# First batch's softmax in four pieces: a bank for each broadcast product, scaling and exp row by row

## The chip, the cores and the metric

The kernel runs on one core of a Trainium2 chip. The metric is the device time of one execution in microseconds (us). TensorE is called PE here, VectorE DVE, ScalarE ACT, GpSimd POOL.

## The reference

Cross-covariance attention over channels, then a gated feed-forward layer. Sizes: 4 batches of 6016 tokens with 256 channels, feed-forward width 1536.

```python
qn = q / (norm(q, axis=1) + 1e-6);  kn = k / (norm(k, axis=1) + 1e-6)
s = kn.transpose(0, 2, 1) @ qn / tau          # 256 x 256 per batch, tau = 1
a = softmax(s, axis=-1)
x = (v @ a).reshape(-1, 256)
out = (sigmoid(x @ w_gate) * (x @ w_val)) @ w_out
```

## The kernel before

The kernel never forms x. It multiplies the softmax matrix into w_gate and w_val once per batch (the twelve "gh products" below, giving the weights G and H) and feeds v to those. For batches 1 to 3 all this runs beside the feed-forward matmuls of the batch before. For the first batch nothing is there to hide it: its softmax is a relay between engines, at about 35 us, right after the last q and k have been loaded.

```python
def spread_k(b):                      # norms of k, as a row on all partitions
    s["rk"] = pso.tile([P, C], FP32, tag="o", name="ps_rk")     # one PSUM bank
    for j in range(CB):               # CB = 2 blocks of 128 columns
        mm(s["rk"][:, ds(j * P, P)], s["r"][:, CB + j : CB + j + 1].to_broadcast([P, P]), ident_f, True, True)

def scale_k(b, i):                    # DVE: both norms at once
    for j in range(CB):
        x = s["x"][:, j, ds(i * P, P)]
        nc.vector.scalar_tensor_tensor(out=x, in0=x, scalar=s["r"][:, j : j + 1],
            in1=s["rk"][:, ds(i * P, P)], op0=ALU.mult, op1=ALU.mult)

def exps(b, i):                       # ACT: one exp of 256 columns per block
    nc.scalar.activation(out=e, in_=s["x"][:, :, ds(i * P, P)], func=ACT.Exp, bias=shift)
...
busy(3); spread_k(0); busy(1); scale_k(0, 0); scale_k(0, 1)
transpose_v(0, 0, ...); exps(0, 0); exps(0, 1); nc.scalar.copy(*late.pop())
sums(0, 0)                            # PE: row sums; DVE: reciprocal
gh(0, 0, psg, "g", act=False)         # even products read w_gate, odd ones w_val
gh(0, 1, psv, "v", act=True)
sums(0, 1, pss, "s")
gh(0, 2, psg, "g", act=False); gh(0, 3, psv, "v", act=True)
gh(0, 4, pso, "o", act=False)
...
for f in range(FC):                   # first chunk of the feed-forward
    glu(0, 0, f)                      # PE: ps_gate, ps_val
    if f < len(gh_order) - 5:
        gh(0, 5 + f, pso, "o")        # two banks, also used by ps_rk
```

`busy` issues matmuls that nobody reads; they keep PE running. Cuts are marked by "...".

## Time and profile before

| | before |
|---|---|
| time, median of 3 | 831.61 us (831.45 to 831.82) |
| span of the profiled execution | 829.8 us |
| first ps_rk record starts | 35.26 us |
| first ps_gate starts | 39.45 us, 4.19 after ps_rk |
| last eviction on DVE starts | 826.14 us, 790.88 after ps_rk |

The last three rows are times in the trace. I count from the first ps_rk record, because what lies ahead of it (when the last k tile lands) differs by some tenths between executions and has nothing to do with the change. The lines of gh product 0, of the first ps_gate and of the last eviction (start, length, engine, line, operation):

```profile
37.25 0.38 PE L88 MATMUL ps_gh<-w_gate,e_sb 128*128 128x512 bf16 x1
...
39.45 0.75 PE L88 MATMUL ps_gate<-vT,gh_G 128*128 128x512 bf16 x2
...
826.14 0.42 DVE L437 COPY out_sb<-ps_o 128x256 f32<-128x256 f32 x1 [0.89 <-PE ps_o L88]
```

Two things in this trace that the prediction doesn't show turned out to matter. The first are instructions in order of time at 42 us (start, length, engine, line, operation):

```profile
42.40 0.69 ACT L364 ACTIVATE gh_G<-ps_gh,rrow 128x512 bf16<-128x512 f32 x1
42.46 0.74 DVE L366 TENSOR_SCALAR gh_H<-ps_gh,rrow 128x512 bf16<-128x512 f32 x1
42.63 0.59 PE L88 MATMUL ps_val<-vT,gh_H 128*128 128x512 bf16 x2
...
43.25 0.59 PE L88 MATMUL ps_gh<-w_val,e_sb 128*128 128x512 bf16 x2
```

A pair of such matmuls follows the pair before it 0.43 us later when PE waits for nothing. Gh product 7 (the last line) could have started at 42.63 + 0.43 = 43.06. It started at 43.25, right after the DVE eviction of product 5 ended (42.46 + 0.74 = 43.20): a bubble of 0.19 us that no list of waits shows. The second is the issue of the first load of w_val, on POOL's queue:

```profile
30.68 0.71 POOL L139 DMA_DIRECT2D w_val<-in_moe_w_val_dram  x1 [0.51 <-DMA q_sb<-in_q_dram]
```

It takes 6.8 us from issue to landing, so it lands at 37.48. Product 1, which reads it, starts at 37.68. The load has 0.2 us to spare.

### The profile page before, as it was taken

Reading aid. Unit: us, or ns where it says so; the run is one execution under the profiler, and the core shown is the slowest. Engines: PE = TensorE matmul, PEld = TensorE weight load, DVE = VectorE, ACT = ScalarE, POOL = GpSimd, SP = SyncE. Lnnn points to the kernel's source line nnn. Section 1 sums busy time; section 2 is a strip of 40 time slices with the busy share of each in tenths; the row PEclk is TensorE's granted clock in tenths of the full one; section 3 lists DMA queues with packets and bytes.
Section 4 is the critical chain, followed back from the end, with each engine's and each line's share of the span. In section 5 each row is a group of like instructions: output and inputs, shape, how many; then the busy total and the mean of one; then the engine's idle time right before and its main releaser. Section 6 shows DMA issues by size and latency. Waiting matters only on the chain.

```text
span 829.8 us, 13778 instructions
## 1 busy us (share of the span) xinstructions
PE 816.5 (98%) x5210; PEld 503.4 (61%) x5224; DVE 580.9 (70%) x998; ACT 391.0 (47%) x642; POOL 83.2 (10%) x159
## 2 busy tenths in 40 slices
PE   7899999999999999999999999999999999999998
PEld 4546666666666666665576666666566566666666
DVE  6677777777667777777767777777766666666664
ACT  4554444445644444444654444444555444444442
POOL 5532100002110100000210020000000000000000
PEclk9999999999999999999999999999999999999999
DMA  9999723326755543223874453233222323322111
GB/s 209 206 206 185 134 52 90 50 62 128 138 105 104 102 108 60 53 52 82 158 140 99 84 110 78 51 77 65 61 59 64 72 51 83 70 49 70 46 36 71
DMA packets 78739, 77.19 MB, mean 93 GB/s; under 512 B 50768, under 2 KB 55632, under 8 KB 78672
## 3 DMA queue, kind: packets, MB, share of 16 engines
q0 software_dynamic: 23920, 38.81, 28.3%
q1 hardware_dynamic: 54608, 36.97, 17.1%
q8 instruction: 41, 0.67, 0.3%
q10 hardware_dynamic: 144, 0.52, 0.2%
q14 instruction: 26, 0.21, 0.1%
HBM read 78.64 MB, written 24.64 MB: 124 GB/s over the span
## 4 chain that ended last, share of the span: by engine, by line
PE 95%; DMA 3%; issue 0%; POOL 0%; DVE 0%; ACT 0%; POOLq 0%; ACTq 0%
PE ps_o L88 30%; PE ps_gate L88 29%; PE ps_val L88 29%; PE ps_s L88 4%; DMA k_sb<-in_k_dram 3%; PE ps_gh L88 2%; PE ps_n L88 0%; POOL q_sb L97 0%; PE ps_busy L88 0%; DVE hT L411 0%; PE ps_rk L88 0%; DVE x_sb L296 0%; ACT g_sb L410 0%; POOL k_sb L97 0%; ACT e_sb L309 0%
## 5 line engine op out<-in xcount | busy, mean ns | idle before, releaser
L411 DVE TENSOR_TENSOR hT<-ps_val,g_sb 128x512 bf16<-128x512 f32 (+1 forms) x576 | 391.2, 679 | 214.9 <-ACT g_sb L410 209.7
L410 ACT ACTIVATE g_sb<-ps_gate 128x512 bf16<-128x512 f32 (+1 forms) x576 | 338.2, 588 | 386.7 <-PE ps_gate L88 378.4
L88 PE MATMUL ps_gate<-vT,gh_G 128*128 128x512 bf16 (+1 forms) x1152 | 337.7, 375 | 0.6 <-ACT g_sb L410 0.4
L88 PE MATMUL ps_val<-vT,gh_H 128*128 128x512 bf16 (+1 forms) x1152 | 337.5, 375 | 0.1
L88 PE MATMUL ps_o<-w_out_sb,hT 128*128 128x256 bf16 x2256 | 326.2, 273 | 0.0
L88 PEld LDWEIGHTS <-hT 128*128 128x128 bf16 x2256 | 220.7, 98 | 124.8
L88 PEld LDWEIGHTS <-gh_H 128*128 128x128 bf16 x1152 | 112.7, 98 | 131.0 <-issue 0.4
L88 PEld LDWEIGHTS <-gh_G 128*128 128x128 bf16 x1152 | 112.4, 98 | 38.0 <-issue 0.6
L106 POOL DMA_DIRECT2D v_sb<-in_v_dram x48 | 25.6, 533 | 624.1 <-DMA vT<-v_sb 501.2
L437 DVE COPY out_sb<-ps_o 128x256 f32<-128x256 f32 x188 | 77.6, 413 | 13.5 <-PE ps_o L88 13.5
L88 PE MATMUL ps_s<-k_sb,q_sb 128*128 128x256 bf16 x376 | 66.0, 272 | 6.1 <-DMA k_sb<-in_k_dram 4.4
L88 PEld LDWEIGHTS <-q_sb 128*128 128x128 bf16 x376 | 36.6, 98 | 14.7 <-issue 6.8
L215 DVE TENSOR_TENSOR acc<-acc,sq 128x1024 bf16<-128x1024 bf16 (+1 forms) x66 | 44.1, 669 | 0.0
L176 DVE TENSOR_TENSOR sq<-q_sb 128x1024 bf16<-128x1024 bf16 (+2 forms) x44 | 29.3, 667 | 2.6 <-DMA q_sb<-in_q_dram 2.6
L97 POOL DMA_DIRECT2D q_sb<-in_q_dram x48 | 26.5, 551 | 15.2 <-DMA q_sb<-in_q_dram 6.5
L97 POOL DMA_DIRECT2D k_sb<-in_k_dram x48 | 26.3, 547 | 13.8 <-DMA k_sb<-in_k_dram 10.2
L176 DVE TENSOR_TENSOR sq<-k_sb 128x1024 bf16<-128x1024 bf16 (+2 forms) x34 | 22.4, 658 | 0.9 <-ACT sq L174 0.9
L364 ACT ACTIVATE gh_G<-ps_gh,rrow 128x512 bf16<-128x512 f32 x21 | 14.4, 687 | 12.4 <-PE ps_gh L88 8.5
L174 ACT ACTIVATE sq<-k_sb 128x1024 bf16<-128x1024 bf16 (+1 forms) x11 | 11.2, 1018 | 14.7 <-DMA k_sb<-in_k_dram 11.9
L88 PE MATMUL ps_busy<-ones_wide,ones_bf 128*128 128x512 bf16 x57 | 16.1, 408 | 1.7 <-DVE shift L127 1.6
L366 DVE TENSOR_SCALAR gh_H<-ps_gh,rrow 128x512 bf16<-128x512 f32 x22 | 16.4, 743 | 1.6 <-PE ps_gh L88 1.6
L460 DVE TENSOR_TENSOR acc<-acc,sq 128x1024 bf16<-128x1024 bf16 x16 | 11.1, 692 | 5.7 <-ACT sq L174 5.4
(58 smaller groups left out, 114.7 us busy)
## 6 DMA issues: line engine op xcount, KB each, us to landing
out_dram<-out_sb SPq DMA_DIRECT2D x44, 512.0 KB, 2.9
v_sb<-in_v_dram POOLq DMA_DIRECT2D x44, 256.0 KB, 3.9
q_sb<-in_q_dram POOLq DMA_DIRECT2D x43, 256.0 KB, 7.0
k_sb<-in_k_dram POOLq DMA_DIRECT2D x43, 256.0 KB, 7.8
out_dram<-out_sb SPq DMA_DIRECT2D x4, 384.0 KB, 2.5
w_gate<-in_moe_w_gate_dram POOLq DMA_DIRECT2D x3, 256.0 KB, 6.8
w_val<-in_moe_w_val_dram POOLq DMA_DIRECT2D x3, 256.0 KB, 7.4
w_out_sb<-in_moe_w_out_dram POOLq DMA_DIRECT2D x1, 768.0 KB, 12.6
```

The source lines that it names most:

```text
L88: nc.tensor.matmul(out, lhsT=lhsT, rhs=rhs, start=start, stop=stop, **kw)
L97: nc.gpsimd.dma_start(out=tl[:, :nt, :], in_=rows(src, b)[:, t0 : t0 + nt, :])
L106: nc.gpsimd.dma_start(out=v_sb[:, :nt, :], in_=rows(v, b)[:, t0 : t0 + nt, :])
L174: nc.scalar.activation(out=sq[:, :nt, :], in_=src[:, :nt, :], func=ACT.Square)
L176: engine.tensor_tensor(out=sq[:, :nt, :], in0=src[:, :nt, :], in1=src[:, :nt, :], op=ALU.mult)
L215: nc.vector.tensor_tensor(out=acc[:, :nt, :], in0=acc[:, :nt, :], in1=st[b]["sq", w][:, :nt, :], op=ALU.add)
L364: nc.scalar.activation(out=dst, in_=ps, func=ACT.Copy, scale=r)
L366: nc.vector.tensor_scalar(out=dst, in0=ps, scalar1=r, scalar2=None, op0=ALU.mult)
L410: nc.scalar.activation(out=g_sb[:, :n], in_=ps_gate[:, :n], func=ACT.Sigmoid)
L411: nc.vector.tensor_tensor(out=hts[b, ci][:, f, :n], in0=ps_val[:, :n], in1=g_sb[:, :n], op=ALU.mult)
L437: nc.vector.tensor_copy(out=out_sb[:, s, :], in_=ps)
L460: nc.vector.tensor_tensor(out=acc[w], in0=acc[w], in1=sq[w], op=ALU.add)
```

## The change

Intent: let DVE begin when the first half of the broadcast is there, and ACT when the first of four scalings is there. Each block's broadcast goes to a bank of its own; DVE multiplies by k's norms alone (tensor_tensor), and q's norm becomes the scale operand of an exp of 128 columns.

```diff
-    def spread_k(b):
-        s["rk"] = pso.tile([P, C], FP32, tag="o", name="ps_rk")
-        for j in range(CB): mm(s["rk"][:, ds(j * P, P)], ...)
+    def spread_k(b, i, pl, tag):
+        ps = pl.tile([P, P], FP32, tag=tag, name="ps_rk")
+        mm(ps, s["r"][:, CB + i : CB + i + 1].to_broadcast([P, P]), ident_f, True, True)
+        s.setdefault("rk", []).append(ps)
...
-    def scale_k(b, i): ...            # scalar_tensor_tensor, two norms
+    def weights(b, i):
+        e = attp.tile([P, CB, P], BF16, tag=f"e{i}", name=f"e_sb{i}", bufs=2)
         for j in range(CB):
+            y = attp.tile([P, P], FP32, tag=f"y{i}{j}", name="y_sb")
+            nc.vector.tensor_tensor(
+                out=y, in0=s["x"][:, j, ds(i * P, P)], in1=s["rk"][i], op=ALU.mult
+            )
+            nc.scalar.activation(
+                out=e[:, j, :], in_=y, func=ACT.Exp, bias=shift, scale=s["r"][:, j : j + 1]
+            )
...
-    spread_k(0)
+    spread_k(0, 0, pso, "o")
+    spread_k(0, 1, pso, "o")
     busy(1)
-    scale_k(0, 0); scale_k(0, 1)
+    weights(0, 0); weights(0, 1)
...
-    exps(0, 0); exps(0, 1)
```

(The diff is cut and its short lines are joined; the calls that it moves are all shown.)

More of the change, by code (lines that the diff above doesn't have):

```diff
@@ L270, in norms_inv @@
             )
-    def spread_k(b):
+    def spread_k(b, i, pl, tag):
         s = st[b]
-        s["rk"] = pso.tile([P, C], FP32, tag="o", name="ps_rk")
-        for j in range(CB):
-            mm(
-                s["rk"][:, ds(j * P, P)],
-                s["r"][:, CB + j : CB + j + 1].to_broadcast([P, P]),
-                ident_f,
-                True,
-                True,
-            )
+        ps = pl.tile([P, P], FP32, tag=tag, name="ps_rk")
+        mm(ps, s["r"][:, CB + i : CB + i + 1].to_broadcast([P, P]), ident_f, True, True)
+        s.setdefault("rk", []).append(ps)
     def copy_s(b, j):
@@ L289, in copy_s @@
         nc.vector.tensor_copy(out=s["x"][:, j, :], in_=s["s"][:, j, :])
-    def scale_k(b, i):
+    def weights(b, i):
         s = st[b]
+        e = attp.tile([P, CB, P], BF16, tag=f"e{i}", name=f"e_sb{i}", bufs=2)
         for j in range(CB):
-            x = s["x"][:, j, ds(i * P, P)]
-            nc.vector.scalar_tensor_tensor(
-                out=x,
-                in0=x,
-                scalar=s["r"][:, j : j + 1],
-                in1=s["rk"][:, ds(i * P, P)],
-                op0=ALU.mult,
-                op1=ALU.mult,
-            )
+            y = attp.tile([P, P], FP32, tag=f"y{i}{j}", name="y_sb")
+            nc.vector.tensor_tensor(
+                out=y, in0=s["x"][:, j, ds(i * P, P)], in1=s["rk"][i], op=ALU.mult
+            )
+            nc.scalar.activation(
+                out=e[:, j, :], in_=y, func=ACT.Exp, bias=shift, scale=s["r"][:, j : j + 1]
+            )
+        s.setdefault("e", []).append(e)
+        s.setdefault("rrow", [])
     def exps(b, i):
@@ L482 @@
     busy(3)
-    spread_k(0)
+    spread_k(0, 0, pso, "o")
+    spread_k(0, 1, pso, "o")
     busy(1)
-    scale_k(0, 0)
-    scale_k(0, 1)
+    weights(0, 0)
+    weights(0, 1)
     late = []
@@ L490 @@
     )
-    exps(0, 0)
-    exps(0, 1)
     nc.scalar.copy(*late.pop())
```

## The prediction

> **What bounds the kernel now.** I read the page first, then the chain of waits over the stretch that the change touches, then the list of instructions in order of time there, and last the list of who waited for whom on TensorE over the rest of the run. From the page, the busy shares and the line of TensorE in 40 slices:
> ```profile
> PE 816.5 (98%) x5210; PEld 503.4 (61%) x5224; DVE 580.9 (70%) x998; ACT 391.0 (47%) x642; POOL 83.2 (10%) x159
> ...
> PE   7899999999999999999999999999999999999998
> ...
> PEclk9999999999999999999999999999999999999999
> ```
> The reader is to see that TensorE (PE) is busy for 98% of the span at the full granted clock. Only the first two slices (some 41 us) have room. The edited code runs once, for the first batch; batches 1 to 3 take their softmax through other functions, hidden beside the matmuls of the batch before. So the question is what the few tenths of a microsecond around 35 to 38 us are worth. The chain of waits there, in order of time (start, length, what):
> ```profile
> 34.49 0.67 PE ps_busy L88 x3
> 35.16 0.10 issue
> 35.26 0.69 PE ps_rk L88 x4
> 35.95 0.02 issue
> 35.98 0.62 DVE x_sb L296 x2
> 36.59 0.03 issue
> 36.62 0.52 ACT e_sb L309
> 37.13 0.05 issue
> 37.18 0.20 PE ps_r L88 x2
> ```
> Read it as a relay: the broadcast product (four PE records, two passes for each of two fp32 matmuls), two of the four scalings on VectorE (DVE), the first exp on ScalarE (ACT), then the row sums on PE. The instructions in order of time add what the engines beside the chain do:
> ```profile
> 34.72 1.28 ACT L478 ACT_TABLE_LOAD   x1
> ...
> 35.98 1.12 DVE L296 SCALAR_TENSOR_TENSOR x_sb<-x_sb,r,ps_rk 128x128 f32<-128x128 f32 x4 [0.56 <-PE ps_rk L88]
> ...
> 36.62 1.02 ACT L309 ACTIVATE e_sb<-x_sb,shift 128x256 bf16<-128x256 f32 x2 [0.62 <-DVE x_sb L296]
> 37.02 0.41 DVE L385 COPY vT<-ps_tp 128x512 bf16<-128x512 bf16 x1
> ...
> 37.18 0.20 PE L88 MATMUL ps_r<-ones_bf,e_sb 128*128 128x1 bf16 x2 [0.58 <-ACT e_sb L309]
> ```
> DVE idles 0.56 us for the whole broadcast, ACT 0.62 us for the scalings, PE 0.58 us for the exp. Taken from 34.4 us to the end, the list of waits on PE has two entries only:
> ```profile
> PE ps_r L88 <- ACT e_sb L309: 0.6, 1, 0.6
> PE ps_gate L88 <- ACT g_sb L410: 0.4, 1, 0.4
> ```
> The second (at 52.4 us) hangs on ACT and DVE work that itself starts from this softmax. No DMA is in the list. So I expect whatever is won at 37.18 to go through to the end nearly whole.
>
> **What the Trainium skill says.** "ScalarE: Activation LUTs", section What ACT_TABLE_LOAD costs: an activation with immediate scale and bias takes 186 ns + 0.833 ns an element, each per-partition pointer operand adds about 93 ns, back-to-back ones overlap by about 93 ns, a load takes 1283 ns. The trace agrees: the exp of 256 columns with a pointer bias should take 492 ns and its rows say 492 to 509; both loads near here last 1.28 us; the copy behind the second exp starts at 37.55, 0.09 before that exp's end at 37.64. "VectorE: DVE Perf Modes", section The TRN2 errata: an fp32 tensor_tensor takes (N+151)/0.96 ns. The trace has none of 128 columns, but the 512-column one from PSUM should take 691 ns and shows 689. "PSUM — Partial Sum Buffer", section PSUM bank collisions raise a hardware error: PSUM is guarded by bank. Here both halves of the broadcast share a bank, and the first scaling starts 0.03 us after the last of the four PE records. "Perfetto Trace Analysis", section Optimizing Scalar/DVE Operations: "If Scalar/Vector aren't saturated, but are causing bubbles on other engines, breaking up instructions may allow work to be completed sooner." That is this change's intent; whether the pieces pay is the sum below.
>
> **The change, part by part.** (1) *A bank per block.* The first DVE instruction needs two PE records, not four. They start at 35.26 and the last at 35.67, so some 0.14 apart; the second starts near 35.40 and, at 275 ns, ends at 35.67. DVE, which finished its copy of the scores at 35.42, starts at 35.70 in place of 35.98: **-0.28**. The same matmuls are issued, so PE's work is unchanged.
>
> (2) *tensor_tensor for scalar_tensor_tensor.* The old one shows 341 ns for 128x128, four in 1.12 us, so starts 0.26 apart. The new one by the skill's formula: (128+151)/0.96 = 291 ns, and I take starts 0.25 apart (estimates). The four run 35.70-35.99, 35.95-36.24, 36.20-36.49, 36.45-36.74. The old four ended at 37.10. DVE's next work, its half of the transposed v, comes 0.3 us earlier, off the path.
>
> (3) *Exp row by row.* The scale of q's norm moves from DVE into the exp, as a second pointer. An exp of 128 columns with two pointers: 186 + 93 + 93 + 107 = 479 ns (estimate by the skill's figures), and a queue of them starts every 479 - 93 = 386 ns. The first can start once its piece is there (35.99 + 0.03) and once the table load is done (34.72 + 1.28 = 36.00): 36.02, almost a tie. So ACT runs 36.02-36.50, 36.41-36.89, 36.79-37.27, 37.18-37.66.
>
> (4) *What PE sees.* The first block of exp values is ready at 36.89, not 37.13; with the same 0.05 the row sums start at 36.94, not 37.18: **-0.24**. The relay's terms are -0.28 (bank), -0.32 (one scaling ahead of the first exp, with no second one and a shorter one) and +0.36 (two small exps take 0.87 in place of one of 0.51). The second block is ready at 37.66 against 37.64, 0.02 later; PE wants it after the row sums and four products of the first, at 38.11 - 0.24 = 37.87. So it still waits for nobody there.
>
> (5) *What follows on ACT and DVE.* ACT's half of the transposed v starts at 37.57 (was 37.55) and leaves ACT free at 38.04; the next eviction on ACT started at 38.31, so it is wanted at 38.07: just in time. DVE is done with its copy near 37.1, in time for the reciprocal of the row sums at 37.18. The step that bounds PE next is the eviction of gh_G on DVE (weights of ps_gate waited 0.48 us for it at 39.81); all of that chain starts from the row sums and moves with them. Then the sigmoid table load and everything after move by the same 0.24.
>
> Sum: 831.61 - 0.24 = 831.37; I say **831.4 us**, a gain of 0.03%.
>
> **The rivals.** *ACT takes the bound.* Exp work on ACT grows from 1.02 to 1.64 us, and step 5 leaves 0.03 us of room. If the two pointers cost more, or exps do not overlap, each exp costs 0.09 more in the queue: the first block is ready at 36.98 (-0.15), the second at 37.94, later than PE wants it, and the eviction of the second product is late by some 0.3. Then the gain is nil or a loss of 0.1 to 0.2: 831.6 to 831.8. For it: ACT has no slack here. Against it: the overlap of 0.09 is visible in this trace. *The wait isn't split.* If DVE still starts at 35.98, the first exp starts at 36.30 and the block is ready at 37.17: 0.04 later than now, time 831.6 to 831.7. For it: the table load forbids an exp before 36.00, so part of any earlier start is useless; against it: two tiles in two buffers have separate waits. *A transfer swallows it.* Between 30 and 60 us the DMA engines are busy all the time at 205 GB/s, and the next batch's q and k are read by PE from 58.3 us on. If one of those lands with less than 0.24 us to spare, PE waits and the gain is gone: 831.6. For it: DMA is full until about 83 us. Against it: PE waits for no DMA after 34.4 us, and a load of k lands in 11 us at worst while it is issued about 20 slots of 1.3 us ahead. *More is won*: up to 0.4 if DVE's pieces start closer together and the small exps are shorter than I reckon; the table load stops it there.
>
> **Range and chances.** The three runs before span 0.37 us, more than the gain, so noise in a median (some 0.15) and the rivals weigh alike. Rivals put the time between 831.2 and 831.8; with noise I take **830.9 to 831.8**. A change of 2% would be 16.6 us; all the softmax of the first batch, from the scores' end to the row sums, is about 3 us. So within 2%: 0.99, and 0.005 on each side.
>
> **What the profile of the changed kernel would show.** The broadcast's first reader on DVE at about 35.70 by the clock of the old trace (0.44 after the first ps_rk), and no wait of 0.56. Four TENSOR_TENSOR of about 290 ns. Four exps of about 480 ns, starts 0.39 apart, the first right behind the table load. The idle time of PE ahead of ps_r down from 0.58 to about 0.34, and ps_gate earlier by as much. The list of waits on PE else unchanged. I am wrong if the exps last over 0.55, if the wait for the second block or for the eviction behind it shows up on PE, or if a DMA enters that list; and the arrival of the last k tile (31.64 in this trace) can move by more than the gain from run to run, so that the total may not show what the stretch shows.

## The result, and the profile after

| | before | changed |
|---|---|---|
| time, median of 6 runs each | 831.65 us (831.45 to 831.92) | 831.39 us (831.28 to 832.01) |
| row sums done, product 0 starts, after ps_rk | 1.99 | 1.80 |
| first ps_gate, after ps_rk | 4.19 | 4.02 |
| product 7 starts, after ps_rk | 7.99 | 7.69 |
| ps_gate behind the stall at 52 us, after ps_rk | 17.16 | 16.86 |
| last eviction starts, after ps_rk | 790.88 | 790.58 |

The ratio is 0.9998 with a 95% interval of 0.9985 to 1.0011: the same, within 2% and within noise. (Ratios are the mean time of one kernel's fast runs over that of the other's of the same rounds, so not quite the ratio of the medians.) The total alone can't show a gain of this size. The traces can: from the start of ps_rk to the last eviction the changed kernel is 0.30 us shorter, and a second profile of it, taken later, gave 790.57, 0.01 off the first. From the stall at 52 us to the last eviction each of these executions takes 773.72 us, before and after, to 0.01. The lines of the changed kernel (its first ps_rk record starts at 35.30):

```profile
37.10 0.59 PE L88 MATMUL ps_gh<-w_gate,e_sb 128*128 128x512 bf16 x2
...
39.32 0.73 PE L88 MATMUL ps_gate<-vT,gh_G 128*128 128x512 bf16 x2
...
825.88 0.42 DVE L432 COPY out_sb<-ps_o 128x256 f32<-128x256 f32 x1 [0.89 <-PE ps_o L88]
```

The chain of waits of the changed kernel, in order of time (start, length, what):

```profile
35.30 0.47 PE ps_rk L88 x2
35.78 0.02 issue
35.80 0.30 DVE y_sb L291
36.10 0.02 issue
36.12 0.89 ACT e_sb L294 x2
```

Set beside the chain of the kernel before: two ps_rk records in place of four, one scaling in place of two, two small exps (0.89) in place of one wide one (0.52). The instructions in order of time:

```profile
34.76 1.28 ACT L473 ACT_TABLE_LOAD   x1
...
35.80 0.88 DVE L291 TENSOR_TENSOR y_sb<-x_sb,ps_rk 128x128 f32<-128x128 f32 x4 [0.33 <-PE ps_rk L88]
...
36.12 1.65 ACT L294 ACTIVATE e_sb<-y_sb,shift,r 128x128 bf16<-128x128 f32 x4
...
37.06 0.18 PE L88 MATMUL ps_r<-ones_bf,e_sb 128*128 128x1 bf16 x1 [0.21 <-ACT e_sb L294]
```

DVE's wait for the broadcast fell from 0.56 to 0.33. ACT's first exp starts at 36.12, behind a table load that ended at 36.04, so the load doesn't bind, but nearly. Row sums now wait for each row by itself: the first of the two ran at 36.67, in the shadow of the second exp.

The second group of lines is the one around gh product 7, and it holds what the prediction did not have:

```profile
42.25 0.69 ACT L359 ACTIVATE gh_G<-ps_gh,rrow 128x512 bf16<-128x512 f32 x1
42.33 0.74 DVE L361 TENSOR_SCALAR gh_H<-ps_gh,rrow 128x512 bf16<-128x512 f32 x1
42.48 0.59 PE L88 MATMUL ps_val<-vT,gh_H 128*128 128x512 bf16 x2
...
42.99 0.59 PE L88 MATMUL ps_gh<-w_val,e_sb 128*128 128x512 bf16 x2
```

Product 7 starts at 42.99, before the DVE eviction of product 5 ends (43.07), and 0.05 after the ACT eviction of product 6 ends (42.94). So it no longer waits for product 5. The built programs say why: before, product 7 is in the bank of product 5 (both in bank 4) and its matmul waits on DVE; after, it is in the bank of product 6 (both in bank 4, product 5 in bank 5) and waits on ACT. The code of these products is the same. The buffer allocator chose otherwise because the instructions ahead of them changed. The bubble fell from 0.19 to 42.99 - (42.48 + 0.43) = 0.08.

So 0.30 us are 0.19 from the softmax (product 0: 1.99 to 1.80) and 0.11 from a bank that moved by accident. The experiments test both.

### The profile page after: what moved, and what is told of

It is laid out like the page before. It is cut to its first block, busy times and chain, and to the rows that moved or that the text cites. A ratio compares the mean times of both kernels' runs of the same rounds, so it can differ in the third digit from the quotient of the medians.

```text
span 829.6 us, 13793 instructions
## 1 busy us (share of the span) xinstructions
PE 817.8 (99%) x5224; PEld 503.6 (61%) x5224; DVE 581.1 (70%) x998; ACT 391.9 (47%) x644; POOL 83.3 (10%) x159
## 4 chain that ended last, share of the span: by engine, by line
PE 95%; DMA 3%; POOL 0%; issue 0%; ACT 0%; DVE 0%; POOLq 0%; ACTq 0%
PE ps_o L88 30%; PE ps_val L88 29%; PE ps_gate L88 29%; PE ps_s L88 4%; DMA k_sb<-in_k_dram 3%; PE ps_gh L88 3%; PE ps_n L88 0%; PE ps_busy L88 0%; POOL q_sb L97 0%; ACT e_sb L294 0%; DVE hT L406 0%; ACT g_sb L405 0%; POOL k_sb L97 0%; PE ps_rk L88 0%; PE ps_tp L376 0%
```

## The experiments

My theory after the result: (a) the softmax part gains by the separate bank alone; the row split with two pointer operands gives a little back; (b) the rest is the bubble ahead of product 7; (c) both reach the end in full, unless a load of weights is late. Rivals: the row split carries the gain; the later stall swallows the bubble; a transfer bounds the run. Each kernel was correct, except the one that was wrong on purpose. Before measured 831.57 (first four), 831.80 (next four) and 831.71 us (last three).

| run | median us (low to high) | product 0 | product 1 | ps_gate | bubble ahead of product 7 | last eviction |
|---|---|---|---|---|---|---|
| before | 831.65 (831.45-831.92) | 1.99 | 2.42 | 4.19 | 0.19 | 790.88 |
| changed | 831.39 (831.28-832.01) | 1.80 | 2.24 | 4.02 | 0.08 | 790.58 |
| one bank | 832.27 (831.47-833.01) | 2.01 | 2.44 | 4.22 | 0.08 | 790.79 |
| banks only | 831.65 (831.26-832.83) | 1.76 | 2.25 | 4.03 | 0 | 791.04 |
| before, free bank | 831.46 (831.19-831.54) | 1.98 | 2.41 | 4.19 | 0 | 790.69 |
| delay | 833.18 (833.03-833.27) | 1.72 | 2.15 | 3.92 | 0.08 | 790.49 |
| one pointer, scaling on DVE | 831.58 (831.38-831.68) | 1.67 | 2.22 | 3.99 | 0.22 | 790.68 |
| no shift | 831.34 (831.23-832.07) | 1.61 | 2.23 | 4.00 | 0 | 790.46 |
| changed, free bank | 831.32 (831.26-831.40) | 1.79 | 2.25 | 4.02 | 0 | 790.49 |
| no shift, later products | 832.60 (832.35-833.76) | 1.61 | 2.24 | 4.02 | 0 | 791.74 |
| other weights (wrong) | 831.22 (one execution) | 1.60 | 2.03 | 3.95 | 0.08 | 790.41 |
| gate first | 831.22 (831.07-831.69) | 1.60 | 2.62 | 3.96 | 0 | 790.52 |
| changed, again | 831.35 (831.24-831.71) | 1.79 | 2.25 | 4.03 | 0.07 | 790.57 |

All columns but the first count from the first ps_rk record.

### One bank: the separate bank undone

```diff
-        ps = pl.tile([P, P], FP32, tag=tag, name="ps_rk")
+        if i == 0:
+            s["rk_both"] = pl.tile([P, C], FP32, tag=tag, name="ps_rk")
+        ps = s["rk_both"][:, ds(i * P, P)]
```

> The changed kernel with one part undone: both broadcast products again in one bank; tensor_tensor and four row exps stay. Times are counted from the start of the first ps_rk record. Before: first scaling 0.72, row sums' end-gating start 1.92, first ps_gate 4.19. Changed: 0.50, 1.76 (second ps_r), 4.02. Theory (the separate bank is the only part that gains, the row split gives some back): first scaling 0.72, first exp 1.03, second ps_r 1.95, ps_gate 4.20 to 4.23, i.e. nothing is left of the gain there. Rival (the row split gains by itself): ps_gate clearly under 4.1. Total: theory within 0.2 of before, some 0.2 us over the changed kernel, too small to be told from one total alone.

Measured: first scaling 0.72, first exp 1.04, second row sum 1.97, ps_gate 4.22. The theory holds: with one bank nothing is left of the softmax gain, and the row split by itself costs 0.02 to 0.03. The last eviction is still 0.09 earlier than before, because product 7 had the bank of product 6 here too (bubble 0.08).

Its total, 832.27, is misleading. Two of its four runs took 833.01 us, the other two 831.47 and 831.53. The profiled one is a slow one. The view of stretches shows busy time of each engine, then PEclk, the granted clock of TensorE:

```profile
core 0: us, PE busy (x) PEld busy (x) DVE busy (x) ACT busy (x) POOL busy (x), PEclk, DMA share, GB/s
28.00:31.50 3.50, 2.46 (x43) 1.85 (x42) 1.65 (x3) 1.06 (x1) 1.95 (x3) 1.00 1.16 202
31.50:35.00 3.50, 3.25 (x28) 2.33 (x29) 0.71 (x2) 2.10 (x3) 3.22 (x5) 0.52 1.23 204
35.00:40.00 5.00, 4.39 (x43) 2.69 (x43) 3.38 (x14) 3.82 (x8) 2.78 (x5) 1.00 1.24 205
```

For 3.5 us the clock was halved, and 1.5 us were lost between the last k and ps_rk (5.06 us apart, against 3.57 in other runs). That lies ahead of the edited code. A run of before (833.07, mean clock 0.998), one of banks only (832.83, 0.998) and one of no shift, later products (833.76, 0.997) look the same by time and mean clock; no trace of them was kept. The Trainium skill, "TensorE: Matmul & The Clock Gate", section What's actually happening, describes a gate with two states, half and full clock, that follows PE's activity over windows of some 3.4 us; the half clock and the length agree with this trace (a mean clock of 0.52 over 3.5 us).

### Banks only: the separate bank alone

```diff
-            y = ...; nc.vector.tensor_tensor(out=y, ...)
-            nc.scalar.activation(out=e[:, j, :], in_=y, func=ACT.Exp, bias=shift, scale=...)
+            nc.vector.scalar_tensor_tensor(out=x, in0=x, scalar=s["r"][:, j : j + 1], in1=s["rk"][i], ...)
+        nc.scalar.activation(out=e, in_=s["x"][:, :, ds(i * P, P)], func=ACT.Exp, bias=shift)
```

> The kernel before with one part of the change alone: a bank for each broadcast product; scalings with both factors and exps of 256 columns as before. Counted from the first ps_rk. Theory: first scaling 0.50, exp 1.14, row sums 1.70, so 0.05 earlier than in the changed kernel (second ps_r 1.76); then the DVE copy of the transposed v (until about 1.96) holds the reciprocal of the row sums, so ps_gate about 3.97 to 4.02, as good as the changed kernel. Rival (the row-by-row exps carry the gain): ps_gate near 4.19. The product of gh number 7 is given the bank of number 5 here, so the bubble ahead of it (about 0.19 in the kernel before, 0.08 in the changed one) should be 0.15 or more, and the total some 0.1 over the changed kernel: 831.4 to 831.6.

Measured: first scaling 0.50, exp 1.14, row sums 1.70, product 0 at 1.76, ps_gate 4.03. The bank alone gives all of the softmax gain: its row sums are even 0.06 ahead of the changed kernel's second one, and ps_gate is the same to 0.01. The rival (ps_gate near 4.19) is out. (ps_gate cannot rank the two kernels, because in both the first load of w_val sets it, as the no-shift run shows. Product 0 comes before that load matters: 1.76 here, 1.80 in the changed kernel.) The bubble forecast was missed for a reason that taught more. The list of waits on PE had an entry that no other run had:

```profile
PE ps_gh L88 <- DMA w_val<-in_moe_w_val_dram: 0.4, 1, 0.4
```

The second load of w_val took 8.1 us to land here (7.4 before), and product 5 waited for it. That gave the evictions ahead of product 7 time, so there was no bubble, and the last eviction came at 791.04. A transfer had swallowed the gain in this execution.

### Before with a free bank for product 7

```diff
-                    gh(0, 5 + f, pso, "o")
+                    gh(0, 5 + f, *((psm, "m") if f == 2 else (pso, "o")))
```

> The kernel before with only one thing changed: product number 7 of the gh weights goes to a bank that is free (that of the norms) in place of one whose eviction it waits for. Theory of the second term (in the changed kernel this product got another bank from the allocator, and the bubble ahead of it fell from 0.19 to 0.08): bubble gone, everything behind it 0.19 earlier, so the PE start behind the stall at 52.4 comes 0.19 earlier, counted from ps_rk, and the total 0.2 lower, 831.45. Rival (the bubble is swallowed by the later stall at 52.4 us, which hangs on ACT): the start behind that stall doesn't move, total as before.

Measured: ps_gate 4.19 as before, no bubble, ps_gate behind the stall at 16.97, last eviction at 790.69: exactly 0.19 less than before. The bubble is real and worth its whole length, and the later stall doesn't swallow it. The changed kernel had got 0.11 of this without asking.

### A known delay

```diff
-    busy(3)
+    busy(13)
```

> The changed kernel with ten idle 512-column products more ahead of the broadcast, 2.13 us of PE work that nobody reads: the relay is made later by a known amount. Theory (all that is won or lost ahead of ps_gate goes through to the end): ps_gate, the start behind the stall at 52.4 and the end 2.1 us later, total 833.5. Rival (a transfer or another wait behind it limits the run): total clearly under 833, and if DMA had been just in time, the list of waits on PE would have a DMA entry that vanishes.

Measured: 833.18 us, 1.79 over the changed kernel, not 2.1. From the last k to ps_gate the trace has 9.38 us against 7.59, so 1.79 later; the last eviction is 795.95 after the last k against 794.15, so 1.80. What is lost ahead of ps_gate reaches the end one for one; that every gain does is not shown by this run. The missing 0.34 is where PE had been waiting. In the changed kernel the three idle products start at 34.39, and at 0.215 each PE could have gone on at 35.04; ps_rk starts at 35.30, as the reciprocal that it reads ends at 35.16. So 0.26 of the delay filled a wait. Another 0.08 came back behind it: with PE kept busy the second ps_rk record ends earlier, and the first scaling starts 0.42 after ps_rk, not 0.50.

### One pointer, scaling on DVE

```diff
-            nc.vector.tensor_tensor(out=y, in0=..., in1=s["rk"][i], op=ALU.mult)
-            nc.scalar.activation(out=e[:, j, :], in_=y, func=ACT.Exp, bias=shift, scale=...)
+            nc.vector.scalar_tensor_tensor(out=y, in0=..., scalar=s["r"][:, j : j + 1], in1=s["rk"][i], ...)
+            nc.scalar.activation(out=e[:, j, :], in_=y, func=ACT.Exp, bias=shift)
```

> The changed kernel with the scale by q's norm moved back into DVE (scalar_tensor_tensor) while the exps stay row by row, now with one pointer operand (the shift). Theory (a pointer costs some 0.09 each on ACT, 341 against 283 ns on DVE): exp 0.39 long, the four in about 1.28 us instead of 1.65; from ps_rk: second ps_r near 1.60 against 1.76. But DVE's four scalings and its copy of v then last until about 1.96, so the reciprocal starts there, at the same 1.96 as in the changed kernel, and ps_gate stays at 4.00 to 4.03. Rival (only the exps count): ps_gate near 3.86.

Measured: exps of 386 ns in place of 480, so a pointer operand costs 94 ns. ps_gate came at 3.99 as forecast, but not for the forecast reason. The reciprocal already started at 1.87. PE had product 0 at 1.67, and could have had product 1 at 2.10, but started it at 2.22. Something else held it, which the next run shows. Beside banks only (product 0 at 1.76) this run adds the row split alone, with one pointer in each exp as there: product 0 comes 0.1 earlier. So the split does gain where it adds no second pointer. The last eviction is 0.10 later than in the changed kernel all the same: product 7 started 0.05 after the DVE eviction of product 5 had ended, as in the kernel before.

### No shift

```diff
-                out=e[:, j, :], in_=y, func=ACT.Exp, bias=shift, scale=s["r"][:, j : j + 1]
+                out=e[:, j, :], in_=y, func=ACT.Exp, scale=s["r"][:, j : j + 1]
```

> The changed kernel without the shift in the four exps (softmax is unchanged by it; scores here are at most 1), so one pointer, the scale. Theory: exp 0.39 long, starts 0.295 apart; from ps_rk: second ps_r near 1.56, DVE's copy done near 1.80, reciprocal there, ps_gate near 3.85, 0.17 under the changed kernel; total 831.2 if the second load of w_val has landed, else PE waits for that load (as one profile of the banks-only kernel showed, 0.41) and the gain is lost behind ps_gate. Rival (pointers cost nothing): as the changed kernel, second ps_r 1.76 and ps_gate 4.02.

Measured: product 0 at 1.61, 0.19 earlier than in the changed kernel, just as reckoned; product 1 at 2.23 and ps_gate at 4.00, only 0.02 earlier. PE in order of time, and the issue of the first load of w_val in the same execution:

```profile
30.55 0.71 POOL L139 DMA_DIRECT2D w_val<-in_moe_w_val_dram  x1 [0.52 <-DMA q_sb<-in_q_dram]
...
36.76 0.59 PE L88 MATMUL ps_gh<-w_gate,e_sb 128*128 128x512 bf16 x2
37.38 0.59 PE L88 MATMUL ps_gh<-w_val,e_sb 128*128 128x512 bf16 x2
```

The two pairs are 0.62 apart, not 0.43. The load lands 6.8 us after its issue, at 37.35, and the product starts 0.03 later. In the changed kernel the same load lands at 30.71 + 6.8 = 37.51, and product 1 starts at 37.54, just when PE gets there (37.10 + 0.43). So the change used up the 0.2 us that this load had to spare. In the traces of one pointer, banks only, later products, changed with a free bank and changed again, too, product 1 starts 0.03 after this landing, and in all of these, as before the change, ps_gate comes 1.77 to 1.78 after product 1. In this order of the products no faster softmax moves ps_gate while this load stays where it is.

A further limit stands behind it, and no list of waits shows it. Product 7 has no bubble here, but ps_val of the step before it starts at 42.29, where 41.74 + 0.43 = 42.17 was possible (its ps_gate pair starts at 41.74):

```profile
39.62 1.28 ACT L495 ACT_TABLE_LOAD   x1
...
41.55 0.69 DVE L406 TENSOR_TENSOR hT<-ps_val,g_sb 128x512 bf16<-128x512 f32 x1 [1.44 <-ACT g_sb L405]
...
42.29 0.59 PE L88 MATMUL ps_val<-vT,gh_H 128*128 128x512 bf16 x2
```

It starts 0.05 after DVE has read the ps_val of two steps before (41.55 + 0.69 = 42.24), DVE waited for the sigmoid on ACT, and that for its table load. The traces of one pointer, later products and gate first show the same 0.05. This link is read from the times; no run tests it alone. In the changed kernel the same DVE read ends at 42.41 and ps_val starts at 42.48, so it has 0.02 to spare.

### Changed kernel with a free bank for product 7

The edit is the one made to the kernel before.

> The changed kernel with product number 7 of the gh weights in a bank that is free. Theory: the bubble of 0.08 left ahead of it goes, the start behind the stall at 52.4 comes 16.78 after ps_rk in place of 16.86, and the last eviction 790.50 in place of 790.58. The kernel before gained 0.19 by the same edit, so with it in both, the softmax part alone is left: 790.69 - 790.50 = 0.19. Rival (the term of 0.13 comes from elsewhere): last eviction at 790.58 as in the changed kernel.

Measured: 790.49. With the bubble gone from both kernels, 790.69 - 790.49 = 0.20 is the softmax part alone, where 0.19 was forecast.

### No shift, later products: a miss

```diff
-                if (b, ci) == (0, 0) and f < len(gh_order) - 5:
-                    gh(0, 5 + f, pso, "o")
+                if (b, ci) == (0, 0) and 1 <= f <= len(gh_order) - 5:
+                    gh(0, 4 + f, pso, "o")
```

> Without the shift, and with products 5 to 11 of the gh weights each one step of the feed-forward later, so that the load of w_val has one more microsecond to land and each eviction more time. Theory (the load and the eviction are the next waits): no DMA entry in the waits on PE, no bubble ahead of product 7; last eviction after ps_rk 790.58 - 0.17 - 0.08 = 790.33, total about 831.1. Rival (the new order opens another wait on ACT or DVE): more than 790.58.

Measured: 832.60 us (832.35 to 833.76); the last eviction 791.74 after ps_rk, 1.16 later than in the changed kernel. The rival was right. Waits on PE:

```profile
PE ps_val L88 <- DVE gh_H L361: 1.3, 2, 0.7
```

Moving the products moved their evictions too, and the feed-forward now waits on DVE for weights that it needs at once. The second load of w_val, with 0.06 us to spare in the no-shift trace (landed 4.80 after ps_rk, read by product 5 at 4.86), now had 0.9; the first, which held product 1, held it here too (2.24). So nothing was won and a worse wait came.

### Other weights

```diff
-                w_sb[w][fg][:, j, :],
+                w_sb[0 if (b, n) == (0, 1) else w][fg][:, j, :],
```

> The kernel without the shift, with the first product of the val weights reading the gate weights instead (wrong numbers on purpose), so that it no longer waits for the first load of w_val. In the kernel without the shift that product starts 2.23 after ps_rk though PE is ready at 2.04; the load was issued at 30.55 and landed 6.8 us later, 37.35, and the product started at 37.38. Theory (that load is what the softmax runs into next): the product starts at 2.04 to 2.06, ps_gate at 3.82 to 3.86 in place of 4.00. Rival (PE waits there for a bank or for DVE): 2.23 and 4.00 as before.

On top of no-shift; its numbers are wrong (relative error 0.29). One execution, 831.22 us. PE in order of time, a little later:

```profile
38.12 0.59 PE L88 MATMUL ps_gh<-w_val,e_sb 128*128 128x512 bf16 x2
38.69 0.59 PE L88 MATMUL ps_gh<-w_gate,e_sb 128*128 128x512 bf16 x2
```

Product 1 now runs straight behind product 0 (the trace merges them), and the row sums of the second block come 2.46 after ps_rk, against 2.66. So it was that load. But ps_gate came at 3.95, not 3.82 to 3.86. The lines are products 3 and 4: product 4 could have started at 38.55 and started at 38.69. It reads the second load of w_gate, issued at 31.84 and landed 6.8 us later, at 38.64. The next load holds PE as the one before did: the weights arrive about as fast as PE takes them.

### Gate products first, and the changed kernel again

```diff
     gh(0, 0, psg, "g", act=False)
-    gh(0, 1, psv, "v", act=True)
     sums(0, 1, pss, "s")
     gh(0, 2, psg, "g", act=False)
+    gh(0, 1, psv, "v", act=True)
```

> The kernel without the shift, with the two gate products of both blocks ahead of the two val products, so that the first load of w_val has 0.5 us more to land. Right numbers. Theory: no gap ahead of the first val product; ps_gate at 3.90 to 3.95 after ps_rk in place of 4.00 (some is lost as the second block of exps is wanted 0.6 earlier), last eviction 790.36 to 790.42 in place of 790.46, unless the next load (the second of w_gate or w_val, each 1.25 us after the one before) holds PE instead: then 4.00 again, and that shows that the arrival of the weights paces this stretch. Total 831.2 to 831.3.

> The changed kernel again, in the same rounds as the gate-first kernel, to compare the two and to have a second profile: last eviction 790.58 after ps_rk if nothing but the arrival of k moves between executions; total 831.3 to 831.5, with single executions 1 to 1.5 us longer where the granted clock of TensorE falls in the first 35 us.

Measured in the same rounds: the table's last two rows. There is no gap ahead of the first val product, and ps_gate came at 3.96, 0.04 ahead of the no-shift kernel where 0.05 to 0.10 was forecast: product 4 started at 3.53, the moment at which its load had landed (31.74 + 6.8 = 38.54, product at 38.59). The forecast of the last eviction failed: 790.52 is 0.06 later than no-shift, not 0.04 to 0.10 earlier, and only 0.05 ahead of the changed kernel. What was won was lost at the further limit told under no shift: ps_val ahead of product 7 started at 42.26 in place of 41.66 + 0.43 = 42.09, with the sigmoid table load at 4.54 after ps_rk, against 4.47 in the no-shift trace. No version tried beats the changed kernel clear of noise; the shortest trace of a correct one is no-shift, 790.46, 0.12 less.

## Why the prediction was right

The predicted time was 831.4 us, the measured median 831.39. By its own steps:

- **A bank per block, -0.28.** Right in mechanism, sized 0.06 too high: DVE started 0.50 after ps_rk in place of 0.72. I had taken the ps_rk records as evenly spaced. The first is slow (348 ns, the others 275), so the second ends 0.47 after the first starts, not 0.41. The trace before had this too (347 ns; starts at 0, 0.18, 0.30 and 0.41).
- **tensor_tensor.** Estimated 291 ns and starts 0.25 apart; measured 282 ns and some 0.20 apart (0.88 us for four). What mattered, the time from DVE's start to the first exp, was 0.32 as predicted.
- **Exp row by row.** Estimated 479 ns and 0.386 apart; measured 480 ns, and 1.65 us for four gives 0.39. Predicted +0.36, measured by the chains 0.89 - 0.52 = +0.37.
- **What PE sees, -0.24.** Measured -0.17 for the gating row sum (1.922 to 1.755) and -0.19 for product 0, because the first row sum no longer stands in its way. The bank's 0.06 and the exps' 0.01 are the difference: -0.24 + 0.07 = -0.17.
- **What follows.** ps_gate moved by 0.17, and product 5, which comes after the wait for gh_G and the first ps_val pair, by 0.19 (5.21 to 5.02). It reached the end in full: with the bubble gone from both kernels the last eviction moves by the same 0.19 to 0.20, and a delay of known size came through too (1.79 in, 1.80 out). What I did not have is the bank of product 7, -0.11. That the total fits so well is luck: one term too large and one term missing nearly cancel (-0.24 predicted, -0.30 in the trace), and a median of six runs can't tell the two apart. Nor would the -0.24 have gone through: product 1 would have been ready at 2.42 - 0.24 = 2.18, and the load would have held it to 2.24.
- **A transfer swallows it.** I looked for it in the wrong place, in the next batch's q and k. It is the loads of w_val: the first had 0.2 us to spare, not visible in a list of waits that showed none. The change used just that, and in one execution of a sibling kernel the second load did swallow the gain.
- **ACT takes the bound; the wait isn't split; more is won.** The first two did not come. More was won, but not where I said.
- **Two readings that were off, with nothing resting on them.** A load of k landed in up to 12.8 us between 36 and 120 us, not 11. And what I called four products ahead of the second block's row sums are four matmuls, of gh products 0 and 1.

The executions scatter more than the gain: one profiled run lost 1.5 us to a halved clock in the prologue, which is more than all terms together, and the changed kernel's slowest run (832.01, mean clock 1.0) is not explained.

## What to carry to other kernels

Where two engines hand a tile over in pieces, ask first what the wait is tied to: here all of the softmax gain came from giving each piece its own bank (product 0 at 1.76 with the bank alone, 1.80 with the whole change). Cutting the exps into rows gave 0.03 back with two pointer operands in each, and gained 0.1 where each had one (1.67): count what a piece pays before you cut. Before betting on an earlier start, work out when the data of the next instructions land (issue plus time to landing) and how much they have to spare; a wait list without a DMA entry says only that none was late this time. And when instructions change, compare which buffer each later tile gets: a rotation that shifts can be worth as much as the edit.

## What the Trainium skill lacked or had wrong

- "VectorE: DVE Perf Modes", The TRN2 errata: its formula, which the page checks at 512 and 2048 elements, gives 291 ns for an fp32 tensor_tensor of 128 columns, SBUF and PSUM in; the trace shows 282 ns.
- "ScalarE: Activation LUTs", What ACT_TABLE_LOAD costs: nothing wrong; 479 ns predicted and 480 measured with two pointers, 386 and 386 with one.
- "Perfetto Trace Analysis", Optimizing Scalar/DVE Operations: breaking up instructions "may allow work to be completed sooner". Nothing wrong, and the section names a per-instruction overhead ahead of this sentence. In the one-bank run, with two pointers in each piece, it did not: ps_gate at 4.22 against 4.19 of the unbroken kernel. With one pointer it did: product 0 at 1.67 against 1.76.
- "TensorE: Matmul & The Clock Gate", What's actually happening: its table says the clock falls after an idle window of some 3.4 us; that row alone does not explain this case. In the one-bank run it fell to half at about 31.5 us though PE had been busy for 2.46 of the 3.50 us before, its longest wait from 20 us on being 1.4 us. The changed kernel's trace has a longest wait of 1.4 us there too, was busy for 2.64 of the same 3.50 us, and kept the full clock. What made it fall in some executions only stays open.
- No page that I read gives a cost for an fp32 matmul of 128 columns with its two passes: here 0.47 us from the start of the first record to the end of the second, 0.39 when PE had been kept busy right up to it (one run, the delay: 0.42 less the 0.03 to DVE's start).
